# Another order of work for the first part and the loop of a cross-attention and maxout kernel

## The chip, the cores and the metric

The kernel runs on one core of a Trainium2 chip. The metric is the device time of one execution in microseconds (us); lower is better. One core has five engines, each with its own queue of instructions that it takes strictly in order: PE (matrix products; its weight loads are listed as PEld), DVE (vector work), ACT (activations, copies, casts), POOL (copies, multiplications, and the issue of most transfers) and SP (issue of transfers only). Transfers run on 16 DMA engines. PE writes into PSUM, eight banks of 128 x 512 floats, which DVE and ACT must empty before a bank is used again.

## The reference

There are 8 batches of 8 heads. In each head, 512 rows `x` and 32 rows `state` of 64 numbers attend to each other in both directions:

```python
scores = scale * np.matmul(x, state.transpose(0, 1, 3, 2))   # softmax over the 32 states
xread  = np.matmul(a, state)
scores2 = scale * np.matmul(state, x.transpose(0, 1, 3, 2))  # softmax over the 512 rows
sread  = np.matmul(a2, x)
```

`xread` and `sread` are joined to 544 rows per head, the heads side by side to rows of 512 numbers, 4352 rows in all. Each row then goes through a layer with maxout and a second layer:

```python
h = np.maximum(np.maximum(x @ w1, x @ w2), x @ w3)   # 512 -> 768, three times
out = h @ w_out                                      # 768 -> 512
```

## The kernel before

The kernel never forms `xread`. For each batch it multiplies the states with the three first-layer weights (a matrix called `G`), and then applies the softmax weights to `G`. One batch goes through these steps; the short names are those of the plan below:

- `lx`, `lxg b g`, `lxu`: load the batch's `x`, whole or one half of the heads, cast to bf16 on the way (`lxu`, uncast, through SP; `cxu` casts it on DVE). `lst`: load the states of two batches. `lw m0 m1 i`: load column blocks m0 to m1 (of 128) of weight i. `lwo`: load `w_out`.
- `stc`, `stt`, `stp`: cast the states, transpose them on PE, place them as block-diagonal matrices (`bd`), which `clr` has set to zero.
- `xt`, `xtc`: transpose `x` on PE and copy it out (batches 0 and 1); `xtd`: the same by a transposing transfer from SP (the other batches).
- `sc`, `ex`, `sum`, `wt`: scores on PE, exponentials on ACT, sums and reciprocals on DVE, the weights `a` by a multiplication on POOL or DVE. `at`, `atc` or `atd` turn `a` into `aT`.
- `pad`, `sr`, `srs`, `srt`, `ap`: the other direction (`sread`). `pad` makes a copy of `x` with a column of ones on POOL, `sr` multiplies on PE, `srs` divides on DVE, `srt` is a transposing transfer, `ap` places the result for the last part.
- `g` and `gc` (batches 0 and 1, by block of 128 columns), `gr` and `grc` (the others, by runs of columns): the matrix `G` on PE and its copy out of PSUM by ACT (A), DVE (D) or in halves by both (DA, AD).
- `l1 b m`: first layer, block m of 768/128 = 6: three groups of two matrix products (six instructions), each group in a bank of its own. `m0` copies the first bank out on ACT, `ma` takes the maximum with the second on DVE, `mb` that with the third, also on DVE.
- `l2 b j`: second layer, quarter j of the rows, six matrix products; `l2c` copies the result out by ACT or DVE; `so b j0 j1` stores it.

The order of all this is written out by hand in three strings. `FIRST` is performed once: it brings in the data, does batches 0 and 1 up to their first layers, and the start of batch 2. `EACH` is performed for b = 2 to 6, with numbers counted from b: it does the first layer of b, the second layer of b-1, and the attention and `G` of b+1, and it loads the `x` of b+3. `LAST` does the first layer of batch 7, the rest of the second layers and the 256 rows of `sread`. The names in a plan are called in their order, and each engine gets its instructions in that order; a wait on a semaphore is put in wherever data or a buffer are still in use. An engine that waits holds everything behind it in its own queue, transfers that it issues included: POOL's multiplications, copies and transfers stand in one line, and so do SP's transfers.

Two more strings say which PSUM bank each step takes: `BANKS` for four single banks, `PAIRS` for two pairs of banks (used by `g`, by the long `gr` and by `sc` of a whole batch). They follow the order of the steps. `busy n` are n products of zeros on PE, whose result nobody reads, while it would otherwise wait for data.

The lines that matter: L168 and L179 issue the loads of x halves and of weights, L184 that of `w_out`, L247 is `xtd`, L300 `atd`, L344 `srt`, L349 `ap`; L226 is `stp`, L235 `xt`, L242 `xtc`, L260 `sc`, L267 `ex`, L274 and L276 `sum`, L282 `wt`, L293 and L296 `at` and `atc`, L309 `pad`, L325 `sr`, L361 all products of `g` and `gr`, L379 and L401 and L404 their copies, L414 `l1`, L429 `m0`, L434 `ma`, L438 `mb`, L445 `l2`, L452 `l2c`, L460 the second layer of the last part in column parts, L475 `so`.

Of the kernel before, what the change touches and what calls it, by code (L numbers as in the profile page):

```python
# [15 lines left out]


FIRST = """
    lxu 0 0 S; lst 0 A; zero; stc 0 D; lxg 1 0; ident; busy 1; lst 1 S; busy 2; busy 1; busy 2; busy 1;
    busy 1; clr 0; stt 0; busy 1; busy 2; cxu 0 0 D; stp 0 AD; stc 1 A; lxg 0 1; clr 3; xt 0 0; lxg 1 1;  # L20
    lw 0 1 0; busy 1; lw 0 3 1; xtc 0 0 A; xt 1 0; xones 0; busy 2; busy 1; lw 0 2 2; xtc 1 0 DA;
    sc 0 0; xt 0 1; lw 1 4 0; busy 1; busy 1; clr 1; lw 2 4 2; sc 1 0; ex 0 0; ex 1 0; clr 2; busy 1;
    xtc 0 1 A; xt 1 1; busy 1; busy 1; sum 0 0; busy 1; stt 1; lw 3 6 1; busy 1; sc 0 1; busy 1; ex 0 1;
    xtc 1 1 D; busy 1; sc 1 1; ex 1 1; busy 1; stp 1 A; lxg 2 1; wt 0 0 P; busy 1; xones 1; at 0 0;
    sum 1 0; busy 1; busy 1; sum 0 1; sr 0; busy 1; sum 1 1; g 0 0; wt 1 0 P; g 1 0; gc 1 0 A; wt 0 1 D;
    sr 1; busy 1; srs 0; lxg 2 0; at 0 1; at 1 0; wt 1 1 P; atc 0 0 D; at 1 1; gc 0 0 D; atc 0 1 A;
    lw 4 6 2; srs 1; atc 1 0 A; g 1 1; atc 1 1 D; warm; gc 1 1 A; g 0 1; l1 0 0 1; g 1 2; m0 0 0; g 0 2;
    l1 1 0; gc 0 1 D; gc 1 2 A; l1 1 1; m0 1 0; ma 0 0; mb 0 0; ma 1 0; lw 4 6 0; mb 1 0; l1 0 1; g 0 3;
    m0 1 1; g 1 3; gc 0 2 A; l1 0 2; ma 1 1; l1 1 2; xtd 2; pad 2; m0 0 1; mb 1 1; ma 0 1; m0 0 2;
    lst 3 A; gc 0 3 DA; l1 0 3; m0 1 2; lwo; gc 1 3 A; ones; g 0 5; g 1 4; mb 0 1; ma 0 2; lxg 3 0;  # L30
    m0 0 3; mb 0 2; gc 0 5 A; lst 2 S; ma 1 2; l1 1 3; stc 3 P; m0 1 3; l1 0 5; mb 1 2; g 0 4; gc 1 4 A;
    g 1 5; ma 0 3; l1 1 4; m0 0 5; gc 0 4 A; mb 0 3; ma 1 3; m0 1 4; lxg 3 1; l1 0 4; sc 2 -; gc 1 5 A;
    xtd 3; mb 1 3; gr 2 1024 1280; m0 0 4; gr 2 1280 1792; ex 2 -; grc 2 1280 1792 A; l1 1 5; m0 1 5;
    ma 0 5; stc 2 A; mb 0 5; gr 2 512 1024; gr 2 1792 2304; sr 2; ma 1 4; mb 1 4; ma 0 4; mb 0 4;
    l2 0 3; grc 2 512 1024 A; stt 2; grc 2 1024 1280 D; gr 2 0 512; l2 0 0; l2 0 1; l2 0 2;
    grc 2 1792 2304 A; sum 2 -; l2c 0 0 A; grc 2 0 512 A; ma 1 5; wt 2 - P; srs 2; l2c 0 3 A; stp 2 A;
    mb 1 5; l2c 0 2 D; atd 2; so 0 2 4 P; stt 3; l2c 0 1 A; stp 3 DA; so 0 0 2 A; lx 4;
"""
EACH = """
    gr 1 0 512; gr 1 1792 2304; l2 -1 0; grc 1 0 512 D; l1 0 0; pad 1; srt -2; m0 0 0; sc 1 -; l2 -1 1;  # L40
    grc 1 1792 2304 A; ma 0 0; l2 -1 3; ex 1 -; gr 1 1024 1280; gr 1 512 1024; l2c -1 0 D;
    gr 1 1280 1792; sr 1; l2c -1 1 A; so -1 0 2 P; mb 0 0; l1 0 1; grc 1 1024 1280 A; l2c -1 3 A; xtd 2;
    m0 0 1; l1 0 2; m0 0 2; l1 0 3; sum 1 -; srs 1; grc 1 1280 1792 DA; ma 0 1; l1 0 5; mb 0 1; m0 0 3;
    ma 0 2; ap -2 A; wt 1 - P; mb 0 2; m0 0 5; l2 -1 2; ma 0 3; grc 1 512 1024 A; mb 0 3; l1 0 4;
    ma 0 5; mb 0 5; l2c -1 2 D; atd 1; m0 0 4; so -1 2 4 P; ma 0 4; lx 3; mb 0 4;
"""
LAST = """
    srt 6; l1 7 0; srt 7; l2 6 0; l1 7 2; m0 7 0; l1 7 3; l1 7 4; ap 7 D; m0 7 2; srt 5; ap 6 A; ma 7 0;
# [14 lines left out]
"""  # L63

BANKS = """
# [3 lines left out]
"""  # L69
PAIRS = """  # L70
    0110101010 1010101010 1001010010 1001010010 10
"""


# [601 lines left out]
```

## Time and profile before

| what | us |
|---|---|
| median of 3 runs (lowest, highest) | 153.15 (153.06, 153.94) |
| the profiled execution: its own time | 153.68 |
| its span from first to last instruction | 151.8 |
| PE busy in the span | 146.3 (96%) |
| DVE busy | 115.2 (76%) |
| ACT busy | 85.3 (56%) |
| POOL busy | 54.0 (36%) |

Shares are of the span. The granted clock of PE was 1.00. A line of the profile names the source line, the engine, the operation, the tile written and the tiles read, the shape, and how often it ran. Start times are in us from the start of the span. "Busy" of PE includes the `busy` products on zeros, and ends of matrix products are modelled, so consecutive products overlap in the list. A wait in square brackets is the idle time of the engine in front of the instruction and what ended it.

### The profile page before, as it was taken

The page shows a single profiled execution, that of the slowest core. Times are in us where ns is not written, and L with a number is a line of the kernel's source. Part 1 is how long each engine was busy: PE and PEld are TensorE (multiplying, and loading weights), DVE is VectorE, ACT ScalarE, POOL GpSimd, SP SyncE. Part 2 cuts the span into 40 slices and gives each one's busy share as a digit, 9 for nine tenths or more (in the row PEclk, how much of TensorE's full clock was granted, in tenths as well). Part 3 has the DMA queues.
Part 4 walks back from the last instruction along what each step waited for, and adds up shares of the span by engine and source line. Part 5 has one row for each costly group of instructions (what it writes and reads, how often), then busy time and mean ns, then how long its engine had stood idle before and what let it go on. Part 6 is the DMA issues. An engine that isn't in the chain of part 4 may idle for free.

```text
span 151.8 us, 3628 instructions
## 1 busy us (share of the span) xinstructions
PE 146.3 (96%) x1420; PEld 73.6 (48%) x1434; DVE 115.2 (76%) x202; ACT 85.3 (56%) x147; POOL 54.0 (36%) x73
## 2 busy tenths in 40 slices
PE   6999899999999999999999999999999999999992
PEld 2565343444445443544354435443544445679771
DVE  1598799889257798879887988798879888676354
ACT  0877775878687581758175817582758353331320
POOL 6988517300427604460356045604360100001500
PEclk9999999999999999999999999999999999999999
DMA  4999999995919989999197929981233120200456
GB/s 115 240 195 201 199 197 196 125 205 73 184 37 287 197 108 246 158 227 176 67 165 192 191 81 178 221 181 49 100 138 86 42 105 6 113 25 17 172 180 201
DMA packets 38053, 22.30 MB, mean 147 GB/s; under 512 B 21504, under 2 KB 35840, under 8 KB 38032
## 3 DMA queue, kind: packets, MB, share of 16 engines
q0 software_dynamic: 14672, 13.44, 46.7%
q1 hardware_dynamic: 21920, 6.95, 22.6%
q10 hardware_dynamic: 1440, 1.64, 3.4%
q8 instruction: 12, 0.20, 0.6%
q14 instruction: 9, 0.07, 0.2%
HBM read 15.20 MB, written 8.91 MB: 159 GB/s over the span
## 4 chain that ended last, share of the span: by engine, by line
PE 87%; DMA 7%; POOL 3%; issue 2%; DVE 1%; POOLq 0%
PE pw L414 47%; PE po L445 25%; DMA w<-in_moe_w_dram 7%; PE pg L361 6%; PE po L460 4%; PE ps L260 2%; POOL w L179 2%; PE psr L325 2%; POOL x L168 1%; PE pgh L361 1%; DVE held L520 0%; PE pt L220 0%; PE idle L518 0%; DVE osb L464 0%; POOL ident masks.py:199 0%
## 5 line engine op out<-in xcount | busy, mean ns | idle before, releaser
L414 PE MATMUL pw<-aT,G 128*128 128x512 bf16 x288 | 66.6, 379 | 0.0
L429 ACT CAST t<-pw 128x512 bf16<-128x512 f32 (+1 forms) x54 | 30.4, 562 | 35.5 <-PE pw L414 21.3
L414 PEld LDWEIGHTS <-G 128*128 128x128 bf16 x288 | 27.2, 97 | 33.9 <-issue 2.5
L434 DVE TENSOR_TENSOR t<-t,pw 128x512 bf16<-128x512 bf16 (+1 forms) x54 | 35.3, 654 | 10.2 <-ACT t L429 7.7
L445 PE MATMUL po<-wout,ht 128*128 128x512 bf16 x155 | 39.1, 380 | 0.7
L438 DVE TENSOR_TENSOR ht<-t,pw 128x512 bf16<-128x512 bf16 x48 | 32.9, 686 | 4.1
L445 PEld LDWEIGHTS <-ht 128*128 128x128 bf16 x168 | 15.3, 98 | 19.2 <-issue 2.1
L475 POOL DMA_DIRECT2D out_dram<-osb x12 | 6.9, 574 | 49.4 <-ACT t L429 27.2
L282 POOL TENSOR_TENSOR a<-e,rden 128x1024 bf16<-128x1024 bf16 (+1 forms) x9 | 14.8, 1647 | 11.8 <-DVE rden L276 10.7
L401 ACT CAST G<-pg 128x1024 bf16<-128x1024 f32 (+1 forms) x19 | 17.1, 908 | 0.0
L309 POOL COPY xp<-x 128x1024 bf16<-128x1024 bf16 x12 | 12.3, 1067 | 5.0 <-DMA x<-in_x_dram 5.0
L452 DVE COPY osb<-po 128x512 f32<-128x512 f32 x14 | 9.6, 686 | 5.6 <-PE po L445 5.6
L452 ACT COPY osb<-po 128x512 f32<-128x512 f32 x15 | 8.9, 593 | 5.8 <-PE po L445 5.8
L209 PE MATMUL idle<-zero 128*128 128x512 bf16 x29 | 10.1, 448 | 1.3 <-DVE zero L187 1.3
L361 PE MATMUL pg<-w,bd 64*32 64x512 bf16 (+1 forms) x288 | 10.7, 362 | 0.6 <-DMA w<-in_moe_w_dram 0.6
L274 DVE TENSOR_REDUCE seen<-e 128x32 f32<-128x1024 bf16 (+1 forms) x10 | 10.0, 998 | 0.5 <-ACT e L267 0.4
L267 ACT ACTIVATE e<-ps 128x1024 bf16<-128x1024 f32 (+1 forms) x10 | 8.6, 861 | 1.6 <-PE ps L260 1.6
L401 DVE CAST G<-pg 128x1024 bf16<-128x1024 f32 (+1 forms) x10 | 9.5, 948 | 0.0
L470 POOL DMA_DIRECT2D out_dram<-osb x4 | 2.2, 540 | 19.9 <-ACT osb L464 19.9
L379 ACT CAST G<-pg 128x768 bf16<-128x768 f32 (+1 forms) x10 | 7.7, 772 | 2.4 <-PE pg L361 2.4
L414 PE MATMUL pw<-atp,w 128*128 128x256 bf16 x72 | 8.7, 272 | 0.0
L414 PEld LDWEIGHTS <-w 128*128 128x128 bf16 x72 | 6.9, 98 | 1.5
(71 smaller groups left out, 113.8 us busy)
## 6 DMA issues: line engine op xcount, KB each, us to landing
out_dram<-osb POOLq DMA_DIRECT2D x11, 512.0 KB, 3.1
x<-in_x_dram POOLq DMA_DIRECT2D x4, 512.0 KB, 7.0
x<-in_x_dram POOLq DMA_DIRECT2D x7, 256.0 KB, 9.1
w<-in_moe_w_dram POOLq DMA_DIRECT2D x3, 384.0 KB, 9.9
w<-in_moe_w_dram POOLq DMA_DIRECT2D x4, 256.0 KB, 8.3
wout<-in_moe_w_out_dram POOLq DMA_DIRECT2D x1, 768.0 KB, 10.6
out_dram<-osb SPq DMA_DIRECT2D x3, 256.0 KB, 2.3
osb<-in_x_dram SPq DMA_DIRECT2D x1, 512.0 KB, 4.1
```

The lines of the kernel that those rows point to most:

```text
L209: nc.tensor.matmul(p, zero[:, 0:128], zero, start=True, stop=True)
L274: nc.vector.reduce_sum(out=den, in_=parity(e[b], g), axis=AX.X)
L282: times[c](out=parity(a[b], g).rearrange("p j g s n -> p j (g s) n"), in0=parity(e[b], g).rearrange("p j g s n -> p j (g s) n"), in1=rdens ...
L309: nc.gpsimd.tensor_copy(out=xp[b][:, :, :, g * (D + 1):g * (D + 1) + D], in_=v[:, g])
L361: nc.tensor.matmul(p(s, g), bd(b, 2 * s + g)[64 * g:64 * g + 64, g, :], f(w_sb[64 * g:64 * g + 64, s]), start=True, stop=True, tile_positi ...
L401: copier[c[g]](out=v[:, g:h], in_=p[:, g:h, 0:c1 - c0])
L414: nc.tensor.matmul(pw[i][:, 0:n], lhs(i, k), rhs(k), start=(k == 0), stop=(k == nk - 1))
L429: nc.scalar.copy(out=t0s[b, m][:, 0:n], in_=open_ps["l", b, m][0][:, 0:n])
L434: nc.vector.tensor_max(t1s[b, m][:, 0:n], t0s.pop((b, m))[:, 0:n], open_ps["l", b, m][1][:, 0:n])
L438: nc.vector.tensor_max(ht[b][:, m, :], t1s.pop((b, m))[:, 0:n], open_ps.pop(("l", b, m))[2][:, 0:n])
L445: nc.tensor.matmul(p, ht[b][:, m, j * 128:(j + 1) * 128], wout_sb[:, m, :], start=(m == 0), stop=(m == NM - 1))
L452: copier[c[i]](out=o[:, j, i * w:i * w + w], in_=p[:, i * w:i * w + w])
```

## The change

Only the strings are edited; no function changes. `FIRST` and `EACH` have the same kinds of steps in another order, with other owners of some copies, and `BANKS` and `PAIRS` follow. `LAST` is the same word for word.

In `FIRST` the weights come in other pieces: weight 0 in blocks 0-1, 1-3, 3-6 (before 0-1, 1-4, 4-6), weight 1 in 0-4, 4-6 (before 0-3, 3-6), weight 2 in 0-2, 2-6 (before 0-2, 2-4, 4-6). POOL issues the halves of x and all weights, then `w_out`, then the two halves of batch 3's x, with no `pad` among them; before, `pad 2` stood ahead of `w_out`. On SP, the transposing transfer of batch 2's x now stands ahead of the loads of states 2 and 3. States 1 come through ACT instead of SP, and `ones` is set first of all on POOL. ACT places states 1 (`stp 1`) ahead of the last two exponentials of batches 0 and 1; before, behind them. The weights `a` of batch 2 are multiplied on DVE instead of POOL.

In `EACH`, the matrix `G` is copied out in other shares, `sc` moves ahead of the first `l1`, one `l2` moves between the first `l1` blocks, the last `l2` stands behind the last `l1`, `wt` comes before the two stores, both stores and the load stand at the end, and `ap` moves from ACT to DVE.

```diff
 FIRST = """
-    lxu 0 0 S; lst 0 A; zero; stc 0 D; lxg 1 0; ident; busy 1; lst 1 S; busy 2; busy 1; busy 2; busy 1;
-    busy 1; clr 0; stt 0; busy 1; busy 2; cxu 0 0 D; stp 0 AD; stc 1 A; lxg 0 1; clr 3; xt 0 0; lxg 1 1;
-    lw 0 1 0; busy 1; lw 0 3 1; xtc 0 0 A; xt 1 0; xones 0; busy 2; busy 1; lw 0 2 2; xtc 1 0 DA;
-    sc 0 0; xt 0 1; lw 1 4 0; busy 1; busy 1; clr 1; lw 2 4 2; sc 1 0; ex 0 0; ex 1 0; clr 2; busy 1;
-    xtc 0 1 A; xt 1 1; busy 1; busy 1; sum 0 0; busy 1; stt 1; lw 3 6 1; busy 1; sc 0 1; busy 1; ex 0 1;
-    xtc 1 1 D; busy 1; sc 1 1; ex 1 1; busy 1; stp 1 A; lxg 2 1; wt 0 0 P; busy 1; xones 1; at 0 0;
-    sum 1 0; busy 1; busy 1; sum 0 1; sr 0; busy 1; sum 1 1; g 0 0; wt 1 0 P; g 1 0; gc 1 0 A; wt 0 1 D;
-    sr 1; busy 1; srs 0; lxg 2 0; at 0 1; at 1 0; wt 1 1 P; atc 0 0 D; at 1 1; gc 0 0 D; atc 0 1 A;
-    lw 4 6 2; srs 1; atc 1 0 A; g 1 1; atc 1 1 D; warm; gc 1 1 A; g 0 1; l1 0 0 1; g 1 2; m0 0 0; g 0 2;
-    l1 1 0; gc 0 1 D; gc 1 2 A; l1 1 1; m0 1 0; ma 0 0; mb 0 0; ma 1 0; lw 4 6 0; mb 1 0; l1 0 1; g 0 3;
-    m0 1 1; g 1 3; gc 0 2 A; l1 0 2; ma 1 1; l1 1 2; xtd 2; pad 2; m0 0 1; mb 1 1; ma 0 1; m0 0 2;
-    lst 3 A; gc 0 3 DA; l1 0 3; m0 1 2; lwo; gc 1 3 A; ones; g 0 5; g 1 4; mb 0 1; ma 0 2; lxg 3 0;
-    m0 0 3; mb 0 2; gc 0 5 A; lst 2 S; ma 1 2; l1 1 3; stc 3 P; m0 1 3; l1 0 5; mb 1 2; g 0 4; gc 1 4 A;
-    g 1 5; ma 0 3; l1 1 4; m0 0 5; gc 0 4 A; mb 0 3; ma 1 3; m0 1 4; lxg 3 1; l1 0 4; sc 2 -; gc 1 5 A;
-    xtd 3; mb 1 3; gr 2 1024 1280; m0 0 4; gr 2 1280 1792; ex 2 -; grc 2 1280 1792 A; l1 1 5; m0 1 5;
-    ma 0 5; stc 2 A; mb 0 5; gr 2 512 1024; gr 2 1792 2304; sr 2; ma 1 4; mb 1 4; ma 0 4; mb 0 4;
-    l2 0 3; grc 2 512 1024 A; stt 2; grc 2 1024 1280 D; gr 2 0 512; l2 0 0; l2 0 1; l2 0 2;
-    grc 2 1792 2304 A; sum 2 -; l2c 0 0 A; grc 2 0 512 A; ma 1 5; wt 2 - P; srs 2; l2c 0 3 A; stp 2 A;
-    mb 1 5; l2c 0 2 D; atd 2; so 0 2 4 P; stt 3; l2c 0 1 A; stp 3 DA; so 0 0 2 A; lx 4;
+    ones; lxg 1 0; ident; zero; lst 0 A; clr 1; stc 0 D; lxg 0 1; lxg 1 1; busy 1; busy 2; busy 2;
+    clr 0; busy 1; lst 1 A; lw 0 1 0; lxu 0 0 S; busy 1; xones 1; stt 0; cxu 0 0 D; busy 1; busy 1;
+    stp 0 AD; busy 1; busy 2; xt 0 0; xt 1 0; xones 0; busy 2; stc 1 A; xtc 0 0 A; xtc 1 0 A; busy 2;
+    sc 0 0; xt 0 1; ex 0 0; lw 0 4 1; busy 1; xtc 0 1 DA; lw 0 2 2; sum 0 0; lw 1 3 0; sc 1 0; busy 1;
+    busy 1; lw 2 6 2; xt 1 1; warm; busy 1; stt 1; ex 1 0; stp 1 A; busy 1; sc 0 1; xtc 1 1 D; busy 1;
+    busy 1; busy 1; busy 1; ex 0 1; wt 0 0 P; busy 1; sc 1 1; busy 1; busy 1; sum 1 0; busy 1; busy 1;
+    at 0 0; ex 1 1; lw 3 6 0; lxg 2 1; sr 0; sr 1; wt 1 0 D; g 0 0; g 1 0; sum 0 1; wt 0 1 P; at 0 1;
+    sum 1 1; srs 0; wt 1 1 P; at 1 0; busy 1; clr 2; lw 4 6 1; atc 0 0 A; srs 1; gc 0 0 AD; lxg 2 0;
+    at 1 1; atc 0 1 A; lwo; atc 1 1 D; l1 0 0; g 0 1; atc 1 0 D; g 1 1; gc 1 0 AD; l1 1 0; m0 0 0;
+    ma 0 0; xtd 2; g 1 2; gc 1 1 A; m0 1 0; g 0 2; lxg 3 1; gc 0 1 D; gc 1 2 A; l1 1 1; m0 1 1;
+    gc 0 2 A; mb 0 0; l1 0 1; g 0 3; g 1 3; m0 0 1; ma 1 0; lst 2 S; mb 1 0; l1 0 2; m0 0 2; l1 1 2;
+    ma 1 1; gc 1 3 A; g 0 5; ma 0 1; g 1 4; gc 0 3 A; l1 0 3; m0 1 2; gc 0 5 A; m0 0 3; mb 1 1; l1 1 3;
+    mb 0 1; ma 0 2; mb 0 2; lxg 3 0; gc 1 4 A; g 1 5; g 0 4; ma 1 2; m0 1 3; mb 1 2; ma 0 3; l1 0 5;
+    pad 2; mb 0 3; ma 1 3; stc 2 P; m0 0 5; gc 0 4 DA; mb 1 3; l1 1 4; m0 1 4; lst 3 S; gc 1 5 A;
+    ma 0 5; xtd 3; mb 0 5; ma 1 4; l1 0 4; m0 0 4; gr 2 1024 1280; gr 2 1792 2304; gr 2 1280 1792;
+    l1 1 5; mb 1 4; sc 2 -; ma 0 4; grc 2 1024 1280 D; grc 2 1280 1792 A; mb 0 4; m0 1 5;
+    grc 2 1792 2304 D; l2 0 2; ex 2 -; stc 3 P; clr 3; l2c 0 2 A; l2 0 3; l2 0 0; sum 2 -;
+    gr 2 512 1024; gr 2 0 512; stt 3; l2c 0 3 A; wt 2 - D; l2 0 1; atd 2; ma 1 5; l2c 0 0 D; mb 1 5;
+    stt 2; grc 2 0 512 A; stp 3 D; l2c 0 1 D; so 0 0 2 P; lx 4; grc 2 512 1024 A; sr 2; stp 2 AD; srs 2;
+    so 0 2 4 P;
 """
 EACH = """
-    gr 1 0 512; gr 1 1792 2304; l2 -1 0; grc 1 0 512 D; l1 0 0; pad 1; srt -2; m0 0 0; sc 1 -; l2 -1 1;
-    grc 1 1792 2304 A; ma 0 0; l2 -1 3; ex 1 -; gr 1 1024 1280; gr 1 512 1024; l2c -1 0 D;
-    gr 1 1280 1792; sr 1; l2c -1 1 A; so -1 0 2 P; mb 0 0; l1 0 1; grc 1 1024 1280 A; l2c -1 3 A; xtd 2;
-    m0 0 1; l1 0 2; m0 0 2; l1 0 3; sum 1 -; srs 1; grc 1 1280 1792 DA; ma 0 1; l1 0 5; mb 0 1; m0 0 3;
-    ma 0 2; ap -2 A; wt 1 - P; mb 0 2; m0 0 5; l2 -1 2; ma 0 3; grc 1 512 1024 A; mb 0 3; l1 0 4;
-    ma 0 5; mb 0 5; l2c -1 2 D; atd 1; m0 0 4; so -1 2 4 P; ma 0 4; lx 3; mb 0 4;
+    gr 1 1792 2304; srt -2; gr 1 0 512; l2 -1 0; sc 1 -; grc 1 0 512 A; l1 0 0; l2 -1 1; gr 1 1024 1280;
+    l2c -1 0 A; grc 1 1792 2304 DA; m0 0 0; pad 1; ma 0 0; mb 0 0; gr 1 512 1024; ex 1 -;
+    gr 1 1280 1792; sr 1; l1 0 1; grc 1 1024 1280 A; sum 1 -; srs 1; l2c -1 1 A; m0 0 1; l2 -1 3;
+    l1 0 2; grc 1 512 1024 DA; grc 1 1280 1792 A; m0 0 2; xtd 2; ma 0 1; l1 0 3; mb 0 1; l2c -1 3 D;
+    ma 0 2; m0 0 3; mb 0 2; ma 0 3; l1 0 5; l1 0 4; l2 -1 2; mb 0 3; m0 0 5; ma 0 5; m0 0 4; l2c -1 2 A;
+    wt 1 - P; so -1 2 4 P; ma 0 4; mb 0 4; lx 3; so -1 0 2 P; ap -2 D; atd 1; mb 0 5;
 """
...
```

More of the change, by code (lines that the diff above doesn't have):

```diff
@@ L65 @@
 BANKS = """
[3 rows of a table removed]
[3 rows of a table added]
 """
 PAIRS = """
-    0110101010 1010101010 1001010010 1001010010 10
+    0101101001 0110010011 0101101011 0101101011 01
 """
```

6 rows, old and new, of the table BANKS are left out of this document.

## The prediction

> **What bounds the kernel now.** I read the page's shares first, then busy time by stages, then the chain that ended last. The stages are cut where the chain shows the loop's first products (43.51, then every 15.26 us).
>
> ```profile
> 16.74:43.51 26.77, 26.71 (x271) 11.42 (x272) 19.84 (x34) 20.11 (x33) 7.29 (x10) 1.00 1.06 160
> ...
> 74.03:89.29 15.26, 15.15 (x148) 6.80 (x150) 12.82 (x21) 8.86 (x15) 6.03 (x7) 1.00 0.76 158
> ...
> 5.00:23.00 18.00, 17.24 (x244) 9.21 (x243) 14.95 (x30) 14.11 (x23) 11.59 (x17) 1.00 1.42 197
> ```
>
> Columns: the stage and its length, busy us (count) of PE, PEld, DVE, ACT, POOL, then the clock, the DMA share and GB/s. From 16.74 on PE is busy all the time, at full clock. Its products are the same before and after the change. So the time is: when PE gets going, plus its products, plus its small waits. The chain, in order of time, shows these waits:
>
> ```profile
> 6.79 9.91 DMA w<-in_moe_w_dram
> 16.74 0.52 PE pg L361 x16
> 17.26 1.40 PE pw L414 x6
> ...
> 33.99 0.47 PE ps L260 x16
> ...
> 37.41 0.32 PE po L445
> ...
> 74.10 0.56 PE pg L361 x16
> 74.65 1.40 PE po L445 x6
> 76.06 1.29 PE pw L414 x6
> 77.35 0.47 PE ps L260 x16
> ...
> 80.41 0.23 PE pgh L361 x8
> 80.64 0.43 PE pg L361 x16
> 81.07 0.38 PE psr L325 x32
> 81.46 5.31 PE pw L414 x24
> ```
>
> Six products take 1.29 when nothing holds them. One turn of the loop has 60 of these (36 `l1`, 24 `l2`): 12.90, with 0.56 + 0.47 + 0.23 + 0.43 + 0.38 for the rest, 14.97; the turn takes 15.26. So **0.29 us a turn are waits**: 0.11 in the first `l2` (1.40), 0.15 in the four `l1` blocks in a row (5.31 against 5.16). Five turns hold 1.4 us, all that the loop can give. The front ends at 16.70 by a load of a weight, issued at 6.79.
>
> **The change: the loads.** Up to batch 2's x, the row on POOL holds the same 3,584 KB (five x halves of 256, weights 2,304). Over 5 to 23 us transfers move 197 GB/s, with no gap to be closed; so x of batch 2 lands where it did:
>
> ```profile
> w<-in_moe_w_dram POOLq DMA_DIRECT2D x1, 256.0 KB, 8.5
> 15.39 1.55 POOL L179 DMA_DIRECT2D w<-in_moe_w_dram  x2
> 22.11 3.24 SPq L247 DMA_TRANSPOSE xT<-x  x1
> xT<-x SPq DMA_TRANSPOSE x1, 10.5
> wout<-in_moe_w_out_dram POOLq DMA_DIRECT2D x1, 768.0 KB, 10.6
> ```
>
> The second of the two issues at 15.39 starts at some 16.2 and lands 8.5 later: 24.7. The load that PE waits for first is also as deep in the row: before, `lw 1 4 0` ends 1,920 KB; after, `lw 1 3 0` ends 1,920 KB. `g 0 0` needs 1,664 KB instead of 1,536: 128 KB (131 thousand bytes) at 197 GB/s are 0.7 later, in by some 14.3 to 15.3 (with the 1 us lateness that the load at 16.70 shows against an even row). `ones` at the head costs its memset, some 0.2, hidden behind the state and x loads that go first.
>
> **The front's compute.** ACT now places states 1 ahead of the last two exponentials:
>
> ```profile
> 11.56 1.26 ACT L267 ACTIVATE e<-ps 128x512 bf16<-128x512 f32 x2 [0.50 <-PE ps L260]
> 12.72 1.16 ACT L226 COPY bd<-pt 64x512 bf16<-64x512 bf16 x2
> ...
> 14.15 1.29 POOL L282 TENSOR_TENSOR a<-e,rden 128x512 bf16<-128x512 bf16 x1 [0.40 <-DVE rden L276]
> ```
>
> That puts 1.16 in front of the last exponential. Before, it ended at 12.82; after, at 13.8 to 14.0, since some of the 1.16 falls into an old wait of 0.50. The last multiplication on POOL started 1.33 after the exponential (14.15) and took 1.29; with the same distance it ends at 16.4, before at 15.44. So the last `at` follows at 16.4, and the first `l1` at some 16.6. Before, PE had to do two `g` blocks (0.45) and that `l1` from 16.74, done at 18.66 (17.26 + 1.40). After, `l1 0 0` goes first (16.6 to 18.0, 0.1 of it waiting for half of a G copy) and the `g` blocks follow, done at 18.45. That is **-0.2**, with bounds: -1.0 if the weights `a` come as early as before, +0.9 if each of the delays (1.16) comes through in full.
>
> From there to the loop the same products remain. Before they take 18.66 to 43.51, 24.85. Eleven `l1` and four `l2` are 15 x 1.29 = 19.4; the `g`, `gr`, `sc`, `sr` and `stt` are some 4.3 by the durations above; 1.2 are waits, mostly for PSUM banks that DVE empties late (two maxima of 0.69, by the row of `mb` below, against 1.29 on PE for each `l1`). Following the new order bank by bank I find waits of 0.2 at `l1 0 1`, 0.2 at `l1 0 2`, 0.1 at `l1 0 4`, 0.3 at the first `gr` (behind `mb 1 4`), 0.2 at `l2 0 1` (behind `wt 2`, now on DVE, and `ma 1 5`): 1.0 with small ones. **No gain, no loss; bounds -0.6 and +0.8**.
>
> Batch 2's x is turned from 24.7 on. Before, `sc 2` ran at 33.99; after, the short `gr` runs (0.66), `l1 1 5` (1.29) and the wait of 0.3 stand ahead of it: 33.99 - 0.2 + 2.25 = 36.0, and the first `l2` behind it, 36.5. With 10.5 (its row before) it lands at 35.2, at the least (its issue on SP, 3.24) at some 28; both are hidden. `w_out` goes at once behind x: 786 thousand bytes at 197 GB/s, or its 10.6: 28.7 to 35.3. Both have cover, of 0.8 and 1.2 at the worse end; before, `w_out` was first used at 37.41. If it fails, PE waits the difference.
>
> The Trainium skill, "DMA: Bandwidth & Descriptors", section "Queues, rings and completion order", says that each DMA engine takes turns between its queues, a packet from each; by it the turning of x would share with `w_out` and not stand behind it, and the sum stays. The 10.5 of the row above is longer than that rule alone would make it, so I do not lean on it.
>
> **The loop.** With PE's durations and t = 0 at the turn's first `gr`, the order after gives: `gr` 0 to 0.56, `l2` to 1.86, `sc` to 2.33, `l1 0 0` to 3.63, `l2` to 4.93, the short `gr` to 5.60, `sr` to 5.98, `l1 0 1` to 7.28, `l2` to 8.57, four `l1` to 13.75, `l2` to 15.04. The engines beside it:
>
> ```profile
> L438 DVE TENSOR_TENSOR ht<-t,pw 128x512 bf16<-128x512 bf16 x48 | 32.9, 686 | 4.1
> L274 DVE TENSOR_REDUCE seen<-e 128x32 f32<-128x1024 bf16 x6 | 7.3, 1218 | 0.0
> L401 DVE CAST G<-pg 128x1024 bf16<-128x1024 f32 x5 | 6.1, 1216 | 0.0
> L401 DVE CAST G<-pg 128x512 bf16<-128x512 f32 x5 | 3.4, 681 | 0.0
> L349 DVE COPY atp<-ats 128x128 bf16<-128x128 bf16 x1 | 0.3, 303 | 0.0
> ```
>
> DVE loses one whole G copy (1.22) and one `l2c` (0.68) and gains a half copy (0.68) and `ap` (0.30): 12.82 becomes 11.9. The wait of 0.11 at the first `l2` goes, because its last `mb` is now done before. What is late next: `l2c 3` on DVE frees the bank of `l1 0 3`. Ahead of it stand the maxima of `l1 0 0` (done at 5.3: that block's first copy on ACT ends at 3.8), the sum (1.22), its reciprocal and the `sread` division (some 0.9), a half G copy (0.68), the maxima of `l1 0 1` (1.4) and itself (a 128x512 copy out of PSUM as well, 0.68): 5.3 + 4.8 = 10.1, less some 0.1 by which operations of DVE overlap; needed at 9.87: a wait of 0.15. Behind it the four `l1` run at DVE's pace without more. So a turn takes 15.1 to 15.2; the first one 0.3 longer, because DVE still places states 2 and 3. Five turns: 15.45 + 4 x 15.18 = 76.2, against 76.3. **-0.1; bounds -1.4** (all waits gone) **and +1.8** (rival 1). `wt` on POOL starts when the reciprocal is there, at 7; `aT` is needed at 15.1 + 2.33 = 17.4: 10 us of cover for that and for the transposing transfer.
>
> **The last part** begins with `l1 7 0` where before `l1 6 4` ran; its third bank waits for `mb 6 5`: **+0.1**, bounds 0 and +0.3. All else there is the same.
>
> Sum: 153.68 - 0.2 + 0 - 0.1 + 0.1 = 153.5 for the profiled execution, whose time is 1.9 over its span and 0.53 over the median of 153.15. On the median it is 152.95; because waits that I do not see can only add, I say **153.1**.
>
> **Rivals.**
>
> 1. *Slower: POOL's line makes `sr` wait.* After, the load and both stores stand ahead of `pad`, which `sr` needs at 5.60.
>
> ```profile
> 74.20 0.59 POOL L475 DMA_DIRECT2D out_dram<-osb  x1 [6.82 <-ACT t L429]
> 75.09 0.90 POOL L163 DMA_DIRECT2D x<-in_x_dram  x1 [0.29 <-issue]
> 76.02 2.05 POOL L309 COPY xp<-x 128x1024 bf16<-128x1024 bf16 x2
> 80.03 0.54 POOL L475 DMA_DIRECT2D out_dram<-osb  x1 [1.96 <-ACT osb L452]
> ```
>
> The first store starts when `l2c 2` on ACT is done (0.81 into the turn, and some 0.3 until POOL starts): 1.08 + 0.59 + 0.90 + 0.54 + 2.1 = 5.2. It decides from 0.4 later on. With the gap of 0.29 in the second row after each of the two stores, and a start 0.2 later, `pad` ends at 6.0: 0.4 a turn, five times, 2.0: 155.1. For it: a margin of only 0.4 in every turn. Against: the issues at 74.20 to 80.03 needed no more than 0.6 and 0.9. Chance 0.16.
>    The Trainium skill, "SBUF — State Buffer", section "Who interferes with whom", says that POOL's reads are shut out by a DVE operation with two inputs in SBUF or in a two-port mode. By it `pad` beside the maxima, which read one input from PSUM, would keep its 2.05; the row shows just that beside maxima before, so this does not raise the chance.
> 2. *Slower: x of batch 2 turned too late.* After, `w_out` and batch 3's x are under way when the turning starts; if the turning ends only when `w_out` (10.6) and batch 3's x behind it (524 thousand bytes at 197 GB/s, 2.7) have landed, at 24.7 + 13.3 = 38.0, `sc 2` waits 2.0: 155.1. For: its 10.5. Against: 0.8 of cover even with that 10.5. Chance 0.08.
> 3. *Faster: the waits go.* The front gains 0.8 and the loop 1.0: 151.4. For: DVE has 0.9 less per turn. Against: its sum still stands ahead of the banks. Chance 0.09.
> 4. *It does nothing it says*: `w_out` and batch 3's x were early enough before (at 37.41, where `w_out` was first used, the chain has no wait for it), so loading them sooner frees nobody, and all waits return elsewhere: 153.2. Chance 0.10.
>
> **How the numbers follow.** The forecast has 0.57. Within 1% (about what a measurement of this kernel can tell from no change) is 151.6 to 154.7. Slower by over 1%: two thirds of rival 1, half of rival 2, and 0.05 of the forecast, whose front and last terms can add up to +1.6: 0.20. Faster: most of rival 3: 0.08. Same: 0.72. The range goes from 151.9 (front and loop at half their lower bounds) to 155.1 (rival 1).
>
> **What would show it.** The first long run of `l1` at 16.6 and not at 17.3; `sc 2` without a wait on a transfer; turns of 15.1 to 15.2 between the first `gr`, with `l1 0 3` waiting 0.1 for `l2c 3`; `sr` not waiting for POOL; DVE at 11.9 a turn. A turn over 15.3, or a first `l1` past 17.2, would make the prediction wrong.

## The result and the profile after

| | kernel before | changed kernel |
|---|---|---|
| median of 15 runs each (lowest, highest) | 153.28 us (153.06, 153.94) | 154.02 us (153.78, 154.47) |
| the profiled execution, its span | 153.68, 151.8 | 154.12, 152.2 |

The ratio is 1.0043 with an interval of 1.0032 to 1.0055: the changed kernel is 0.4% (0.74 us) slower. The forecast was no change, with 0.05 us less than the median known then.

The stages of the changed kernel are these: from just ahead of the first layer-1 product (16.30 by its record) to the loop, the loop's first turn, a later turn, and the stretch of the loads (columns as before: stage and length, busy us and count of PE, PEld, DVE, ACT, POOL, clock, DMA share, GB/s):

```profile
16.27:43.51 27.24, 27.16 (x284) 11.42 (x289) 24.40 (x40) 18.60 (x29) 7.01 (x10) 1.00 1.05 159
43.51:59.02 15.51, 15.49 (x157) 6.78 (x164) 13.18 (x25) 9.31 (x16) 5.99 (x7) 1.00 0.86 155
74.32:89.62 15.30, 15.30 (x156) 6.87 (x164) 11.61 (x22) 9.65 (x16) 6.03 (x7) 1.00 0.75 158
5.00:23.00 18.00, 17.98 (x260) 9.77 (x258) 13.86 (x29) 14.45 (x24) 12.35 (x18) 1.00 1.39 199
```

The transfers run as before (199 GB/s against 197) and VectorE (DVE) has 1.2 us less to do in a later turn (11.61 against 12.82), yet that turn takes 15.30 instead of 15.26, and the first one 15.51. The chain that ended last, in order of time, shows where:

```profile
16.47 1.29 PE pw L415 x6
17.76 0.45 PE pg L362 x16
18.21 1.40 PE pw L415 x6
...
29.50 2.28 PE pw L415 x10
31.78 0.20 issue
31.98 0.70 DVE ht L439
32.68 0.04 issue
32.73 0.59 PE pw L415 x2
...
36.24 0.47 PE ps L261 x16
...
49.59 1.42 PE pw L415 x6
51.00 0.01 issue
51.01 1.47 PE po L446 x6
...
74.32 0.56 PE pg L362 x16
74.88 1.40 PE po L446 x6
76.28 0.47 PE ps L261 x16
76.74 1.29 PE pw L415 x6
78.04 1.29 PE po L446 x6
79.33 0.23 PE pgh L362 x8
79.57 0.43 PE pg L362 x16
80.00 0.38 PE psr L326 x30
80.38 1.40 PE pw L415 x6
81.78 1.29 PE po L446 x6
83.08 5.25 PE pw L415 x24
88.33 1.29 PE po L446 x6
```

Three things are to be seen. In the first part VectorE's third maximum (L439) stands on the path from 31.98, behind 0.20 of "issue", a wait that the profile ties to nothing. In the first turn the output product at 51.01 takes 1.47 where it takes 1.29 later (81.78). And in the later turn *two* groups of six take 1.40, each right behind products with 32-column weights (`pg` before 74.88, `psr` before 80.38), while the other single groups take 1.29.

Sixteen profiles were taken in all. Their stages repeat to 0.02 us; mainly the start differs from run to run, while the halves of x land up to 0.7 us apart. So the stages tell more than one run's time does. By the records' start times (up to 0.1 us ahead of the chain's):

| kernel (first part, loop body) | first layer-1 product | from there to turn 1 | turns 1, 2, 3, 4 | median us | ratio to before (interval) |
|---|---|---|---|---|---|
| before, two profiles | 17.19, 16.95 | 26.32 | 15.26 each | 153.28 | 1 |
| changed, three profiles | 16.30, 16.05, 16.74 | 27.13 | 15.52, 15.30, 15.30, 15.30 | 154.02; 153.96 on the later chip | 1.0043 (1.0032 to 1.0055); 1.0035 (1.0016 to 1.0053) |
| h1: new, old | 16.07 | 27.12 | 15.72, 15.25, 15.25, 15.26 | 156.77 | 1.0226 (1.0197 to 1.0255) |
| h2: old, new | 16.90 | 26.32 | 16.25, 15.30, 15.30, 15.31 | 154.72 | 1.0103 (1.0072 to 1.0134) |
| s1 and r2: new + 1 clearing, new | 16.62, 16.19 | 26.68 | 15.52, 15.30, 15.30, 15.30 | 153.85; 153.59 | 1.0033 (1.0013 to 1.0053); 1.0007 (0.9987 to 1.0028) |
| s2: old + 2 clearings, old | 16.58 | 26.45 | 15.25 each | 156.16 | 1.0196 (1.0163 to 1.0228) |
| s3: new with a placing on ScalarE, new | 16.45 | 27.14 | 15.61, 15.31, 15.31, 15.31 | 154.24 | 1.0060 (1.0036 to 1.0084) |
| s4: new + 1 clearing, old | 16.52 | 26.69 | 15.73, 15.49, 15.26, 15.25 | 153.74 | 1.0019 (0.9999 to 1.0038) |
| x1: old, old with `gr` split | 16.90 | 26.3 | 15.52, 15.68, and so on | 155.30 | 1.0132 (1.0094 to 1.0169) |
| x2: new without half a placing, new | 16.04 | 27.1 | 15.31, 15.30, and so on | 154.17 | 1.0051 (1.0028 to 1.0075) |
| v1: new + 1 clearing, `wt 2` on GpSimd, new | 16.51 | 26.55 | 15.30 each | 153.34 | 0.9989 (0.9974 to 1.0004) |
| v2: as v1, old body | 16.39 | 26.55 | 15.27, 15.25, 15.25, 15.25 | 153.38 | 1.0001 (0.9981 to 1.0020) |

### The profile page after: what moved, and what is told of

It is laid out like the page before. It is cut to its first block, busy times and chain, and to the rows that moved or that the text cites. A ratio compares the mean times of both kernels' runs of the same rounds, so it can differ in the third digit from the quotient of the medians.

```text
span 152.2 us, 3632 instructions
## 1 busy us (share of the span) xinstructions
PE 148.0 (97%) x1435; PEld 74.1 (49%) x1435; DVE 113.5 (75%) x208; ACT 86.4 (57%) x148; POOL 52.6 (35%) x73
## 4 chain that ended last, share of the span: by engine, by line
PE 97%; DVE 1%; issue 0%; DVEq 0%
PE pw L415 47%; PE po L446 25%; PE idle L210 6%; PE pg L362 6%; PE po L461 4%; PE ps L261 2%; PE psr L326 2%; PE pxt L236 1%; PE pgh L362 1%; PE pt L221 1%; PE pat L294 1%; DVE ht L439 0%; DVE held L521 0%; PE idle L519 0%; DVE osb L465 0%
## 5 line engine op out<-in xcount | busy, mean ns | idle before, releaser
L435 DVE TENSOR_TENSOR t<-t,pw 128x512 bf16<-128x512 bf16 (+1 forms) x54 | 35.3, 653 | 19.7 <-ACT t L430 17.4
L446 PE MATMUL po<-wout,ht 128*128 128x512 bf16 x168 | 40.6, 379 | 0.0
L439 DVE TENSOR_TENSOR ht<-t,pw 128x512 bf16<-128x512 bf16 x48 | 32.8, 685 | 4.1 <-PE pw L415 0.6
L446 PEld LDWEIGHTS <-ht 128*128 128x128 bf16 x168 | 15.8, 98 | 20.2 <-issue 1.7
L476 POOL DMA_DIRECT2D out_dram<-osb x13 | 7.4, 571 | 45.8 <-DVE ht L439 22.8
L402 ACT CAST G<-pg 128x1024 bf16<-128x1024 f32 (+1 forms) x23 | 18.5, 829 | 5.8 <-PE pg L362 3.3
L453 ACT COPY osb<-po 128x512 f32<-128x512 f32 x19 | 11.2, 591 | 14.1 <-PE po L446 14.1
L283 POOL TENSOR_TENSOR a<-e,rden 128x1024 bf16<-128x1024 bf16 (+1 forms) x8 | 12.6, 1582 | 12.1 <-ACT osb L453 5.0
L210 PE MATMUL idle<-zero 128*128 128x512 bf16 x31 | 10.7, 467 | 1.3 <-DVE zero L188 1.3
L471 POOL DMA_DIRECT2D out_dram<-osb x4 | 2.2, 541 | 18.6 <-ACT osb L465 18.6
L402 DVE CAST G<-pg 128x512 bf16<-128x512 f32 (+1 forms) x11 | 8.0, 729 | 0.0
L453 DVE COPY osb<-po 128x512 f32<-128x512 f32 x10 | 6.9, 686 | 1.4 <-PE po L446 1.3
```

The source lines that it names most:

```text
L210: nc.tensor.matmul(p, zero[:, 0:128], zero, start=True, stop=True)
L283: times[c](out=parity(a[b], g).rearrange("p j g s n -> p j (g s) n"), in0=parity(e[b], g).rearrange("p j g s n -> p j (g s) n"), in1=rdens ...
L402: copier[c[g]](out=v[:, g:h], in_=p[:, g:h, 0:c1 - c0])
L435: nc.vector.tensor_max(t1s[b, m][:, 0:n], t0s.pop((b, m))[:, 0:n], open_ps["l", b, m][1][:, 0:n])
L439: nc.vector.tensor_max(ht[b][:, m, :], t1s.pop((b, m))[:, 0:n], open_ps.pop(("l", b, m))[2][:, 0:n])
L446: nc.tensor.matmul(p, ht[b][:, m, j * 128:(j + 1) * 128], wout_sb[:, m, :], start=(m == 0), stop=(m == NM - 1))
```

## The experiments

### The same two kernels again

> The kernel before, unchanged, profiled a second time. Its first profiled execution took 153.68 us with a span of 151.8, 0.4 above its median of 153.28, and the changed kernel's median is 0.74 above that of before while the spans differ by only 0.4. Theory (the two profiles hide 0.3 to 0.4 us of the loss, because that execution of before was itself long): this execution takes 153.0 to 153.4 and its span is 151.1 to 151.5, with the missing 0.3 to 0.4 us in one nameable place. Rival (the span is always about 151.8 and what lies outside it varies): the span is again 151.7 to 151.9.

> The changed kernel, unchanged, profiled a second time. In its first profile VectorE's third maximum of sixth 5 of batch 0 (L439) begins at 31.98, 0.5 us after everything that it waits for, and the layer-1 products behind it on TensorE wait 0.2, 0.4 and 0.3 us in a row. Theory (the order and the bank numbers of the new first part make this wait): it is there again at the same place, 0.8 to 1.0 us of waits on TensorE between 31.8 and 33.9. Rival (an accident of that execution): it isn't there, the first turn of the loop begins 0.5 to 0.9 earlier than 43.5, and the time is below 153.6.

Both were unchanged. The kernel before took 153.45 with a span of 151.54, both just above what the theory expected: its first layer-1 product came at 16.95, not 17.19, since the weight that landed at 16.70 in the first profile landed at 16.08 now. From there on all is the same to 0.01. So the first profile of before was 0.24 long, at one nameable place. The changed kernel took 153.78, and VectorE's late maximum was there again, 31.73 for 31.98 with everything 0.25 earlier. It was no accident.

### Each new part with the other old one

```diff
 # h1: FIRST as in the changed kernel; h2: FIRST as before
-EACH of that kernel
+EACH of the other kernel, bank digits 0 and 1 exchanged from the loop on
```

> The new first part with the old loop body (bank numbers renamed where the two meet). Theory (the loss lies in the new loop body, 76.70 instead of 76.29 us for its five turns, and the new first part is worth about 0.1): 0.3 to 0.5 us less than the changed kernel, 153.5 to 153.7, a ratio to the kernel before of 1.000 to 1.003, and turns of 15.26 with none of 15.5. Rival (the loss is what the new first part leaves for the first turn, two state blocks still to be placed and a half of G still to be copied when the loop begins): the first turn stays at 15.45 to 15.55, the other four go back to 15.26, and the ratio is 1.003 to 1.005.

> The old first part with the new loop body. Theory (the loss lies in the loop body): a ratio to the kernel before of 1.002 to 1.004 (0.3 to 0.6 us), the first turn 15.4 to 15.5 and the others 15.30. Rival (the first turn's extra comes from the new first part): the first turn too is 15.30, five times 0.04 make 0.2 us, and the ratio is 1.001 to 1.002.

Both theories missed most of it: each mixture is slower than either kernel. The later turns belong to the body (15.25 and 15.30), but the first turn belongs to the pair: 15.26 and 15.52 where first part and body were written for each other, 15.72 and 16.25 where not. In h2 the scores wait until 46.09 for a copy of G on ScalarE behind a state placing; in h1 until 46.80 for one on VectorE. And h1 lost another 2.6 us at its very end, where VectorE took 3.08 us from its last branch to the next instruction; 0.49 to 0.52 in the others.

### VectorE's 64th instruction

```diff
 # s1 and r2, in the new FIRST
-lst 0 A; clr 1; stc 0 D;
+lst 0 A; clr 1; clr 1; stc 0 D;
 # s2, in the old FIRST
-lst 0 A; zero; stc 0 D;
+lst 0 A; zero; clr 0; clr 0; stc 0 D;
```

> The changed kernel with one more clearing of state block 1 on VectorE (0.49 us, at about 1.8 us, where VectorE waits for the first states anyway), so that all later VectorE instructions move up by one number. In all five profiles so far the 64th recorded VectorE instruction begins 0.51 to 0.53 us after the 63rd, whatever the two are: in the kernel before it is a second maximum that would have begun 0.12 earlier, in the changed kernel a third maximum that would have begun 0.47 earlier. Theory (the step from the 63rd to the 64th instruction costs 0.5 us of its own, and the changed order has put it where nothing hides it): the step now falls between the second maximum of sixth 5 and the wait behind it, which comes 0.7 us later anyway; the third maximum begins 0.07 instead of 0.53 us after its wait, the waits of 0.2 and 0.2 us on TensorE behind it shrink, the loop begins 0.3 to 0.7 us earlier, and the median falls to 153.3 to 153.7. Rival (the order or the bank numbers make that wait): all stays within 0.1 us of the changed kernel.

> The kernel before with two more clearings on VectorE ahead of the first state cast, where VectorE is idle; nothing else. Theory as above: the 64th VectorE instruction is now a third maximum that stands right behind its wait, it begins about 0.45 us later than in the kernel before, and the loop begins 0.2 to 0.5 later. Second theory, on the 3.08 us that VectorE took in the hybrid with the new first part and the old loop from its last branch to the next instruction (0.49 to 0.52 in the four other kernels), there with the branch as the 320th recorded instruction: here the branch is the 320th again, so that jump takes about 3.1 us and the whole run 156.0 to 156.7. Rival (neither depends on the number of an instruction): 153.2 to 153.4, both steps as before.

The timeline of VectorE around its 64th recorded instruction, waits counted too (columns: start, length, engine and line, shapes, idle time before and what seems to have ended it). The kernel before:

```profile
30.17 0.69 DVE L438 TENSOR_TENSOR ht<-t,pw 128x512 bf16<-128x512 bf16 x1
30.98 0.69 DVE L434 TENSOR_TENSOR t<-t,pw 128x512 bf16<-128x512 bf16 x1
```

The changed kernel:

```profile
30.74 0.68 DVE L435 TENSOR_TENSOR t<-t,pw 128x512 bf16<-128x512 bf16 x1
31.98 0.69 DVE L439 TENSOR_TENSOR ht<-t,pw 128x512 bf16<-128x512 bf16 x1 [0.57 <-PE pw L415]
```

The changed kernel with one clearing more (s1), and the kernel before with two (s2):

```profile
31.05 0.68 DVE L435 TENSOR_TENSOR t<-t,pw 128x512 bf16<-128x512 bf16 x1
31.84 0.69 DVE L439 TENSOR_TENSOR ht<-t,pw 128x512 bf16<-128x512 bf16 x1
```

```profile
28.77 0.69 DVE L434 TENSOR_TENSOR t<-t,pw 128x512 bf16<-128x512 bf16 x1 [0.28 <-ACT t L429]
30.00 0.69 DVE L438 TENSOR_TENSOR ht<-t,pw 128x512 bf16<-128x512 bf16 x1 [0.55 <-PE pw L414]
```

The row with 0.57 names TensorE, but the products it reads ended at 30.9, and ScalarE had by 31.37 passed a wait for later ones. A maximum normally begins 0.1 after the one it needs; here it is 0.57. One cheap instruction more ahead of it, and the gap is 0.11 (31.05 + 0.68 to 31.84). Two more in the kernel before, and it has the same gap of 0.55, at another maximum. In all eleven profiles whose 63rd record is a wait, the 64th begins 0.51 to 0.53 after it. In the kernel before, 0.4 of that lay beside the maximum at 30.17 (0.12 was idle); in the changed kernel all of it is bare. From the first layer-1 product to the loop it is worth 0.45 us (27.13 to 26.68), more than half of the loss. In s2 it cost only 0.13 (26.32 to 26.45), less than the 0.2 to 0.5 expected; why it costs less there is not shown.

s2 also has VectorE's branch as its 320th record, as h1 has, and the jump took 3.27 us. So the second theory holds as well, and its 2.8 us are the whole of s2's loss.

The same step is there at the 192nd recorded instruction, three times 64. The reciprocal of the fourth turn is the 192nd in the kernel before (first two rows) and the 194th in s2 (last two):

```profile
94.24 1.22 DVE L274 TENSOR_REDUCE seen<-e 128x32 f32<-128x1024 bf16 x1
95.94 0.35 DVE L276 RECIPROCAL rden<-seen 128x32 f32<-128x32 f32 x1 [0.47 <-DVE seen L274]
...
93.75 1.22 DVE L274 TENSOR_REDUCE seen<-e 128x32 f32<-128x1024 bf16 x1
95.07 0.35 DVE L276 RECIPROCAL rden<-seen 128x32 f32<-128x32 f32 x1
```

As the 192nd it begins 0.48 after the end of the sum that it needs, as the 194th 0.10. It costs nothing here, since the next reciprocal waits for TensorE until 96.76 anyway.

On the path from this to the median, s1 was too noisy: 153.85, on another chip and with x landing late. So:

> The changed kernel beside the next one on one chip, since the first layer-1 product began between 16.05 and 16.62 us in the six profiles with the new first part (it follows the second x block by 7.71 to 7.74 us, and that lands between 8.0 and 8.6), which is as much as the differences looked for. Expected: 0.6 to 0.9 us over the kernel before, a ratio of 1.004 to 1.006, and 27.13 us from the first layer-1 product to the first turn, turns of 15.52 and 15.30, as in the two profiles before.

> The changed kernel with one more clearing early on VectorE, again, beside the changed kernel on one chip. Theory (the 64th VectorE instruction costs the changed kernel 0.45 us, as the first part showed: 26.68 instead of 27.13 us): the median is 0.3 to 0.5 us below that of the changed kernel. Rival (the 0.45 us come back further on, or the clearing costs as much at the start): within 0.15 of it.

On one chip 153.96 became 153.59, 0.37 less, within the 0.3 to 0.5 that was expected.

### The first turn

```diff
 # s3
-stp 2 AD; srs 2;
+stp 2 A; srs 2;
 # x2, in states_place: VectorE's half of block 2 is left out
-for i in range(2):
+for i in range(1 if k == 2 else 2):
 # v1, on top of s1
-wt 2 - D;
+wt 2 - P;
```

> The changed kernel with both halves of the last placing of state block 2 on ScalarE; the second of them took VectorE 0.70 us at 44.65. Theory (the first turn of the loop is 0.2 us longer than the others because VectorE starts it behind with the placing of the states): ScalarE is idle from 43.75 to 44.14, VectorE comes 0.7 us earlier to the state read-out and the half of G, the first turn falls from 15.51 to 15.30 to 15.40, and the median by 0.1 to 0.2. Rival (something else, such as the copies of G on ScalarE, delays the first turn): the turn stays at 15.5 or grows by the 0.2 us that ScalarE's copy of G comes later.

> The changed kernel without VectorE's half of the last placing of state block 2 (0.70 us at 44.65; batches 4 and 5 then run with half of their state heads at zero, so this part of the work is left out). Theory (the first turn's extra 0.2 us: VectorE is late with the state read-out of batch 2 and its half of G, so ScalarE's half of G and the maxima come late, then the sums, then the read-out of batch 3, whose bank the output product at 51.01 waits for): the first turn falls to 15.30 to 15.36, the others stay at 15.30, and the median falls by 0.15 to 0.25. Rival (ScalarE's copies of G set the first turn, as moving the placing there made it 15.61): 15.5.

> The changed kernel with one more clearing early on VectorE, as in the last call, and with the weighting of batch 2 on GpSimd again, where the kernel before has it (there 1.91 us); in the changed kernel it takes VectorE 1.23 us at 39.57, while GpSimd is idle from 36.6 to 44.9. Theory (the first turn is long because VectorE brings a backlog into it; the run without half of a placing brought that turn to 15.30): the weighting ends 0.6 us later, the transposing transfer behind it still lands by 45.0, ahead of the layer-1 product at 45.8 that needs it, VectorE is ahead by up to 1.2 us, the first turn is 15.30 to 15.36, the other turns 15.30, and the median 0.1 to 0.25 below the 153.59 of the last call: 153.3 to 153.5, a ratio to the kernel before of 0.998 to 1.001. Rival (the transfer behind the weighting lands too late and takes the place of the backlog): the first turn stays at 15.5 or grows.

The timeline of the changed kernel, VectorE and ScalarE in its first turn:

```profile
44.65 0.69 DVE L227 COPY bd<-pt 64x512 bf16<-64x512 bf16 x1
45.79 0.68 DVE L402 CAST G<-pg 128x512 bf16<-128x512 f32 x1
46.50 0.58 ACT L402 CAST G<-pg 128x512 bf16<-128x512 f32 x1 [0.41 <-DVE G L402]
46.98 0.59 ACT L430 CAST t<-pw 128x512 bf16<-128x512 f32 x1
47.61 0.69 DVE L435 TENSOR_TENSOR t<-t,pw 128x512 bf16<-128x512 bf16 x1 [1.14 <-ACT t L430]
49.00 1.21 DVE L275 TENSOR_REDUCE seen<-e 128x32 f32<-128x1024 bf16 x1
50.66 0.29 DVE L342 TENSOR_TENSOR sr<-psr,seen 128x128 bf16<-128x128 f32 x1
```

Each row waits for the one above or stands behind it: the placing at 44.65 delays VectorE's half of G, ScalarE's half waits for that, the first copy of the layer-1 block stands behind it, then the maxima, the sum, and at 50.66 the division that frees the bank of the output product at 51.01. Moving the placing to ScalarE (s3) moved the delay, for ScalarE's copies of G stand in the same chain: 15.61. Leaving it out (x2) brought the turn to 15.31, though the median of that run, 154.17, didn't fall; why is open. v1 shows where the backlog came from: with the weighting of batch 2 back on GpSimd, which was idle there, every turn is 15.30. Of v1's chain, the same groups as at 49.59 and 51.01 above:

```profile
49.19 1.40 PE pw L415 x6
50.59 1.29 PE po L446 x6
```

The transfer behind the weighting landed at 44.02, in time. The first part also became 0.13 shorter (26.68 to 26.55), and the median is that of the kernel before: 153.34 against 153.37.

### The 0.11 us behind narrow weights

```diff
 # x1, in the old EACH
-gr 1 0 512; gr 1 1792 2304; l2 -1 0;
+gr 1 0 512; l2 -1 0; gr 1 1792 2304;
```

> The kernel before with its loop body in one point another: the first output product of the turn stands between the two wide products of G that open the turn, no longer behind both; nothing is added. Each turn of every profile has a group of six full products at 1.40 instead of 1.29 us right behind products with 32-column weights. Theory (0.11 us is what TensorE itself takes when it goes from 32-column weights to full ones, not a wait for another engine, so that the prediction's 0.29 us of waits a turn were only 0.07): one more such place in each turn, a layer-1 group at 1.40, turns of 15.37 instead of 15.26, and a median 0.5 to 0.7 above the kernel before. Rival (the 0.11 us are a wait for a bank or a copy): the first copy of G begins 0.2 earlier, the waits shrink, turns of 15.15 to 15.26.

The chain of x1 in its second turn:

```profile
58.81 0.34 PE pg L361 x8
59.15 0.97 PE po L445 x4
60.12 0.02 issue
60.14 0.60 PE po L445 x2
60.74 0.34 PE pg L361 x8
61.08 1.40 PE pw L414 x6
62.48 0.47 PE ps L260 x16
```

The layer-1 group at 61.08 stood behind full products before and took 1.29; behind narrow ones it takes 1.40, as forecast. Both semaphores that this group waits for had been set by 59.55, 1.5 us ahead of it, so it waited for no other engine. The rival, a shorter turn, is out. But the price of one more change of weights is larger than I said: the sixteen products of G, 0.56 in one go, take 0.34 + 0.34 in two, so going *to* narrow weights costs another 0.12. With 0.04 in the output group the first turn is 0.26 longer. From the second turn on the output product also comes too early for its maxima: 0.97 + 0.02 + 0.60 is 1.59, 0.19 over 1.40. So 15.52 and 15.68 instead of 15.37.

The Trainium skill, "TensorEngine Tiling (Array Packing)", section "Key Properties", says that a change of the tiling mode drains TensorE. The trace agrees (the products of G use tiles of 64 x 32, those behind them 128 x 128), and adds the price: 0.11 to 0.12 us each way.

### The old body behind the mended first part

```diff
 # s4: h1 with s1's clearing; v2: also v1's weighting, and one clearing more behind VectorE's 64th record
+clr 1;
-wt 2 - D;
+wt 2 - P;
+clr 3;
```

> The new first part with the old loop body once more, with one more clearing on VectorE early, which moves VectorE's branch from the 320th to the 321st place and its 64th instruction off the third maximum. Theory of numbers: the last jump takes 0.5 instead of 3.08 us, the first part 0.3 to 0.7 less, and the median falls from 156.8 to 153.4 to 153.9; the first turn stays at about 15.7 and the others at 15.26, so the old loop is then no better behind the new first part than the new one. Rival (the hybrid is slow for another reason, such as its lower granted clock): above 155.5.

> The new first part mended as in the last run (one clearing early, weighting of batch 2 on GpSimd) with the old loop body; one more clearing on VectorE at about 37.6, where it is idle for 0.25 us, keeps VectorE's branch at the 321st place. Theory (the turns of 15.73 and 15.49 of that hybrid were the same backlog of VectorE, and the old body is 0.04 us a turn shorter than the new one where nothing is handed over): five turns of 15.25 to 15.26, 0.2 us less than the last run, a median of 153.1 to 153.3 and a ratio to the kernel before of 0.996 to 1.000. Rival (the old body needs the hand-over of the old first part, with the scores later in the turn): a first turn of 15.4 to 15.7 again, and a ratio of 1.000 to 1.003.

s4 confirms both place numbers at once: the jump took 0.52, the first part 26.69, the median 153.74. In v2 the turns of 15.73 and 15.49 are gone (15.27 and 15.25), so they were the backlog too. The old body is 0.04 us a turn shorter than the new one behind the same first part. The median of v2, 153.38, is just above the 153.1 to 153.3 that was expected, and can't be told from v1's or from that of the kernel before: no version here beats both.

## Why the prediction was wrong

**The account.** Five profiles with the old first part have their first layer-1 product at 16.90 on average (16.58 to 17.19), eleven with the new one at 16.35 (16.04 to 16.74). The new order does that product ahead of two `g` blocks (0.45) that stood before it, so on equal work the front gains 0.10 and the middle, 27.13 against 26.32, loses 0.36. The first turn adds 0.26, the next three 0.12, the fifth with the last part 0.04. Together +0.68, beside +0.74 and +0.62 by the medians of the two comparisons.

- **Loads: right in time.** x of batch 2 landed at 24.67 (24.7 forecast), `w_out` at 28.46 (28.7 to 35.3), the turned x at 33.73 (28 to 35.2), and `sc 2` ran at 36.24 (36.0) without a wait. Rival 2 is out as a loss, but its mechanism was half there: the turning, issued at 24.75, moved its first packet at 28.78, behind `w_out`, and ended behind batch 3's x (32.40); only, all this was 4 us earlier than the rival's 38.0. So the rule on queues that the prediction takes from the Trainium skill ("DMA: Bandwidth & Descriptors", "Queues, rings and completion order") is seen here only beside batch 3's x, not beside `w_out`; why is open.
- **Front, -0.2: right** as far as can be told, -0.10 on average with starts that differ by 0.6 to 0.7 from run to run; the last `at` ran at 16.07 and the first `l1` in the chain at 16.47 (16.4 and 16.6 forecast).
- **"No gain, no loss" from there to the loop: wrong by 0.36.** This step failed. Without VectorE's 64th instruction the middle is 0.09 shorter than before, but that the rest came out near nothing was partly luck, for the waits followed bank by bank aren't the ones that came. In s1, `l1 0 1` and `l1 0 2` don't wait (each pair of blocks takes 2.70, 1.40 behind narrow weights and 1.29); the 0.3 at the first `gr` is 0.2 (0.44 against 0.23 in the loop), and the 0.2 at `l2 0 1` is 0.14 (1.43) and the weighting's doing (1.29 in v1). Of the 1.2 us put down to waits for banks in the kernel before, some 0.8 are the price of narrow weights (seven groups behind them, 0.11 each: an estimate). The step of the 64th instruction was in no sum, because in the profile of before only 0.12 of it shows, and that beside other work.
- **"0.29 us a turn are waits": the step that failed in the loop.** 0.22 of it were two changes from narrow to full weights, which both bodies have; true waits were 0.07. So there was nothing to win, and the forecast of 15.1 to 15.2 came to 15.30. The 1.2 us less on VectorE, forecast as 12.82 to 11.9 and measured as 11.61, bought nothing. The wait forecast at `l1 0 3` isn't there: the four `l1` take 5.25, 0.09 over 4 x 1.29, in two small waits at `l1 0 5` and `l1 0 4`.
- **The first turn, 15.45: near in size**, 15.52 measured, **by half of the cause**. I named the placing of states, and without half of it the turn is 15.31 (x2); v1 shows that the weighting moved to VectorE was what made it matter. I had priced that move only at `l2 0 1` of the first part.
- **Last part, +0.1**: not there, 0.0.
- **Rivals 1 and 3 are out**: `sr` stands 5.68 after the turn's start (80.00 - 74.32) with no wait for GpSimd's copy, and no wait went. Rival 4 is half right: loading `w_out` and x earlier freed nobody, but the rest of the order did cost something.

Two costs, 0.45 for the 64th instruction and 0.35 for the weighting (0.22 in the first turn, 0.13 ahead of it), are the whole of the loss; without both the new order ties with the old.

## What to carry to other kernels

A pause that has the same length in every turn and always stands behind the same kind of instruction may be the engine's own price and not a wait to be won: test it, and take it out before summing waits. A new order also moves work to other places in an engine's count of instructions; a gap that no wait explains is tested by adding one cheap instruction far ahead of it. And an operation moved to an engine near the seam of two stages is priced in the stage behind the seam, where that engine's backlog ends.

## What the hardware did that I hadn't expected

- VectorE's 64th recorded instruction begins 0.51 to 0.53 us after its 63rd (eleven profiles where the 63rd is a wait). The 192nd begins 0.44 after its 191st in the three profiles where that is a wait for the sum just ended, against 0.06 to 0.07 where the same reciprocal has another number. At the 256th nothing shows (0.18 behind a wait in the changed kernel). What happens there isn't shown. The Trainium skill, "Advanced Engine Details and Errata", section "ISA Cache", gives lines of 256 instructions, which does not explain a step at 64, and no transfer of instructions lies at that moment (the nearest begins at 33.84 in the changed kernel).
- VectorE's last branch took 3.08 and 3.27 us to the next instruction in the two kernels where it was the 320th record (five times 64), and 0.49 to 0.52 in fourteen profiles where it was the 313th to 318th or the 321st. One clearing more, which made it the 321st, saved 2.6 us (h1 to s4, 3.08 to 0.52).
- Going from 32-column weights to full ones costs TensorE 0.11 us, and going back 0.12.
- The second half of x lands between 7.9 and 8.6 us from run to run, and the new front moves with it, though not one for one: 8.00, 8.01 and 8.40 in the changed kernel, with first layer-1 products at 16.30, 16.05 and 16.74. That is as much as the whole change.
